# A state-space convolution and a gated feed-forward layer on one core: dummy matmuls at the start, first loads on two queues, memsets off GpSimd, a 78-row tile, another order

## The chip, the cores and the metric

The kernel runs on one core of a Trainium2 chip. The core has a matrix engine (TensorE, in the profile PE for matmuls and PEld for weight loads), a vector engine (VectorE, DVE), a scalar engine (ScalarE, ACT), GpSimd (POOL) and a sync engine (SyncE, SP) that mostly issues DMAs. Each engine takes its instructions in program order and waits on semaphores for the others. SP, ACT and GpSimd each have a DMA queue. Matmuls read SBUF and write PSUM; here PSUM is used as four double banks of 128 x 2 x 512 fp32, called banks 0 to 3 below.

The metric is the device time of one execution in microseconds (us), as the median of the runs. Before the change it was 275.33 us (three runs, 275.13 to 275.48).

## The reference

For `x` of 2048 x 640 (bf16) the kernel computes `g * a + (1 - g) * b`:

```python
g = sigmoid((x * gate_w).sum(-1, keepdims=True))
a = ssm_conv(x)          # u below is x
b = (gelu(x @ w_gate) * (x @ w_up)) @ w_down   # 640 -> 1728 -> 640

def ssm_conv(u):
    dt = exp(log_dt)[:, None]                  # 640 channels, 128 states each
    P = exp(dt * (A_re + 1j * A_im) * l)       # for each lag l = 0 .. 2047
    K = einsum("dn,dnl,dn->dl", C, P, dt * B).real
    y = irfft(rfft(pad(K)) * rfft(pad(u)))     # causal convolution along the length
    return y + u * Dskip
```

The lags are rounded to bf16 in the reference, and the kernel uses that: only a few distinct lags are left above 256.

## The kernel before

The kernel is one long hand-made schedule. Each piece of work is registered under a short name by `step(name, fn)`, and the string `ORDER` (lines 39 to 91) lists all 984 names in the order in which they are emitted. Since every engine takes its own instructions in the order of emission, `ORDER` fixes the order on each engine and on each DMA queue. A name with `/0` to `/3` opens a matmul job in that PSUM bank, and a name with `/A` or `/D` says whether ACT or DVE evacuates the bank. A job that opens in a bank waits until the readers of the job before it in that bank are done.

What the names stand for, in the rough order of the work:

- *Parameters.* `lp0` to `lp5` load A_re, A_im, C_re, C_im, B_re, B_im (L272), `ldt` the log step sizes (L268), `lpk` a constant table `picks` with an identity, two flipped identities and an edge table (L267). `t0` to `t5` turn the six parameters with ten small matmuls each (L312: the parameter is the stationary operand, 64 columns of the identity move). `tdt` (L318) spreads the log step sizes over the partitions with a matmul of one row. `dt` (ACT, L332) is the exponential of that; `al`, `al2` and `th` (DVE, L334, L335, L337) are the scaled real and imaginary exponents; `c2`, `c3` (ACT, L341) copy C out of PSUM, and `v0` to `v18` and `mag` combine B, C and A into the coefficient of each state, in magnitude and angle.
- *Tables of powers*, once for each half of the channels (suffix `.0` and `.1`). `xa`, `xb` are exponentials on ACT (L470, L472, L480, L484). `fa`, `fb`, `qa`, `qb` are phases on DVE (L492, L500, L487), `sa`, `sb` sines on ACT (L504, L507), `ma`, `pa`, `pc`, `pb` products on DVE. `oa` and `ob` are memsets of ones in these tables, `fil` two fills. `ct0.0` to `ct0.6` contract the tables over the states on PE (L537, L538), and `ek` steps unload the result. `ks`, `kd`, `kt` add the skip term and regroup the kernel samples through DRAM.
- *Gate and up products.* For each half of the length (`.0`, `.1`) there are 27 jobs `g`, `u` and `h` of ten matmuls with 512 columns (L391). In the first half the first four `g` and `u` jobs of the first two weight slots are cut by the five tiles of x (`g0.0`, `g0.0k1` to `g0.0k4`), so that they can run as the transposing loads `x0.0` to `x4.0` (L287) land. `lw0g`, `lw0u` and so on load the weights (L280). `eg`, `eu` evacuate, `su`, `sg` store to DRAM, because the results are needed only later. `hz0`, `hz1` set the lower half of the last tile of H to zero (GpSimd memsets of 64 x 1024, L622 and L630), which must follow the store `su13.0` of what lay there.
- *Folds.* `ul`, `ur` load chunks of x forwards and backwards (`ur` with GpSimd's indirect DMA, L375), `uf` adds and subtracts them (L382).
- *Spectra.* `U` and `K` jobs are the forward transforms of x and of the kernel (L729, L742), `m`, `s`, `y` the products on DVE (L788, L790, L791), `I` the inverse transform (L802).
- *The end.* `ge`, `dg` are gelu on ACT (L709, L712, L680); `rl`, `hm` reload the up products and multiply. `D` jobs are the down product, 14 tiles of rows deep (L816), `Z` mixes in the convolution (L823, L824), `o` scales and writes out (L402, L404), `st` stores. `lwz0`, `lwz1` are GpSimd memsets that clear rows 64 to 127 of the last tile of the down weights, and `lwe` writes fourteen edge rows into it. `gf` flips the gate with a table in `picks`.
- *Dummies.* `wm0` to `wm2` at the very end run two matmuls each on `picks` (L296), while the last stores are under way.

The head of the order, and its end, before:

```
lpk lp3 t3/2 ldt lp0 one tdt/1 tabE dt c3 lp5 t0/0 al lp2 t2/1 xa11.0 c2 al2 xb5.0 xb9.0 lp4 xa17.0 xb14.0 lw0g t5/0 v2 v3
xb23.0 x0.0 t4/1 g1.0/3 xa3.0 sk v0 v4 lp1 xb2.0 lw0u xa8.0 xb31.0 xb8.0 x1.0 v1 v5 v6 t1/0 th g0.0/2 u1.0/1 fb1.0 g0.0k1
x2.0 u0.0/0 idx xb21.0 g1.0k1 qb1.0 v7 xa16.0 x3.0 v8 v11 xb11.0 xa9.0 u0.0k1 u0.0k2 x4.0 v9 u0.0k3 g0.0k2 fb0.0 qb0.0 xb10.0
...
D120a D121/0 Z120 o120/A D121a D131/3 Z121 y130 D131a st120 y131 o121/A I131/0 st121 I130/1 eI131/A eI130/A Z131 o1311/D
o1310/A st1311 Z130 o1300/D st1310 o1301/A st1300 wm0/2 wm1/0 st1301 wm2/2
```

Of the kernel before, what the change touches and what calls it, by code (L numbers as in the profile page):

```python
# [39 lines left out]
lpk lp3 t3/2 ldt lp0 one tdt/1 tabE dt c3 lp5 t0/0 al lp2 t2/1 xa11.0 c2 al2 xb5.0 xb9.0 lp4 xa17.0 xb14.0 lw0g t5/0 v2 v3  # L40
xb23.0 x0.0 t4/1 g1.0/3 xa3.0 sk v0 v4 lp1 xb2.0 lw0u xa8.0 xb31.0 xb8.0 x1.0 v1 v5 v6 t1/0 th g0.0/2 u1.0/1 fb1.0 g0.0k1
x2.0 u0.0/0 idx xb21.0 g1.0k1 qb1.0 v7 xa16.0 x3.0 v8 v11 xb11.0 xa9.0 u0.0k1 u0.0k2 x4.0 v9 u0.0k3 g0.0k2 fb0.0 qb0.0 xb10.0
u0.0k4 g1.0k2 v10 xb1.0 xa4.0 u1.0k1 u1.0k2 lw1g xb29.0 ul0 eu0.0/D g0.0k3 xb3.0 u1.0k3 v12 xb15.0 v13 xb12.0 lw1u g1.0k3
u1.0k4 g1.0k4 xa15.0 eu1.0/D g3.0/0 v14 g0.0k4 g3.0k1 g3.0k2 xa14.0 xb7.0 g3.0k3 oa.0 xb17.0 u3.0/1 eg1.0/D ur0 xb6.0 su0.0
eg0.0/D xa10.0 xb19.0 g2.0/3 xa7.0 u2.0/2 xa5.0 x0.1 g3.0k4 v15 xb13.0 xa19.0 g2.0k1 xb4.0 xa1.0 v16 uf0.0 u3.0k1 uf0.1 lw2
xb27.0 xb25.0 u2.0k1 u3.0k2 v17 u2.0k2 g2.0k2 mag ma2.0 eg3.0/A u2.0k3 u3.0k3 fil.0 ma1.0 g2.0k3 su1.0 ur1 u2.0k4 v18 ma3.0
eu2.0/D g2.0k4 x2.1 us0 u3.0k4 lw3 u4.0/0 ma4.0 ma5.0 ma0.0 tabT sb0.0 fb2.0 eu3.0/A su3.0 sb1.0 ul1 pb0.0 pc0.0 eg2.0/A
su2.0 fb3.0 u5.0/2 ob.0 eu5.0/A qb2.0 sb2.0 pb1.0 g5.0/1 pc1.0 eg5.0/A fb4.0 g4.0/3 pc2.0 pb2.0 u6.0/2 eu4.0/A at qb4.0
# [96 lines left out]
def kernel(  # L145
# [125 lines left out]
    for i in range(6):  # L271
        step(f"lp{i}", lambda i=i: (A if i == 0 else S).dma_start(out=at["prm"][:, i],  # L272
                                                                 in_=PRM[i].rearrange("(p j) n -> p (j n)", p=128)))
# [628 lines left out]
```

## Time and profile before

| | |
|---|---|
| median of 3 runs | 275.33 us (275.13 to 275.48) |
| the profiled execution | 275.08 us |
| its span, first to last instruction | 273.3 us |
| busy: PE, DVE, ACT, GpSimd | 261.3, 255.6, 219.4, 36.7 us |
| DMA moved | 49.05 MB, mean 179 GB/s |
| granted TensorE clock, mean | 1.000 |

The profile is of one execution. PE's busy time is modelled, because matmuls are pipelined: a matmul that stands in the profile with 379 ns is followed by the next one after some 0.22 us, so a busy PE is read from the spacing of its instructions. "Idle before" an instruction is the time its engine did nothing before it, with the name of what ended the wait. A name such as `ps` stands for all tiles of that name. SPq, ACTq and POOLq are the engines' instruction queues, where DMAs are issued.

### The profile page before, as it was taken

How to read it: one execution, taken by the hardware profiler on the slowest of the kernel's cores; microseconds unless marked ns; L12 is line 12 of the kernel's file. 1: busy time of each engine (PE TensorE's matmuls, PEld its weight loads, DVE VectorE, ACT ScalarE, POOL GpSimd, SP SyncE). 2: the span in 40 equal slices, each digit the busy share in tenths (PEclk: the TensorE clock that was granted, in tenths of full speed). 3: DMA queues.
4: the chain of work that ended last, by engine and by line, in shares of the span. 5: the costliest groups of instructions: out<-in, count | busy, mean ns of one | idle time of the engine just before them, and what ended most of it. 6: DMA issues, size and time to landing. Idle time of an engine off the chain costs nothing.

```text
span 273.3 us, 4927 instructions
## 1 busy us (share of the span) xinstructions
PE 261.3 (96%) x1874; PEld 159.8 (58%) x1889; DVE 255.6 (94%) x330; ACT 219.4 (80%) x300; POOL 36.7 (13%) x23
## 2 busy tenths in 40 slices
...
GB/s 196 261 184 227 250 140 242 276 208 105 195 272 139 233 265 245 246 287 210 276 288 121 280 252 195 289 202 267 262 246 23 50 0 26 46 2 50 24 50 48
DMA packets 64141, 49.05 MB, mean 179 GB/s; under 512 B 23499, under 2 KB 52982, under 8 KB 64118
## 3 DMA queue, kind: packets, MB, share of 16 engines
...
q8 instruction: 15, 0.25, 0.4%
...
## 4 chain that ended last, share of the span: by engine, by line
PE 71%; ACT 18%; DVE 5%; issue 3%; DMA 2%; SPq 0%; DVEq 0%; ACTq 0%
PE ps L391 24%; PE ps L816 22%; PE ps L802 6%; PE ps L729 6%; PE ps L742 4%; ACT work L396 3%; DVE work L398 2%; ACT work L480 2%; PE ps L537 2%; PE ps L538 2%; ACT work L472 2%; ACT H L709 2%; PE ps L823 2%; ACT work L484 2%; PE ps L824 1%
## 5 line engine op out<-in xcount | busy, mean ns | idle before, releaser
L391 PE MATMUL ps<-xT,Wr 128*128 128x512 bf16 x525 | 118.9, 379 | 3.7 <-DVE work L347 0.7
L391 PEld LDWEIGHTS <-Wr 128*128 128x128 bf16 x540 | 52.6, 98 | 65.7 <-issue 5.0
L396 ACT CAST work<-ps 128x640 bf16<-128x640 f32 (+1 forms) x59 | 47.5, 838 | 11.5 <-PE ps L802 7.4
L375 POOL DMA_INDIRECT early<-in_A_u_dram,back x8 | 31.4, 3929 | 40.7 <-DVE early L382 32.3
L816 PE MATMUL ps<-xT,H 128*128 128x320 bf16 x224 | 32.9, 299 | 0.0
L402 ACT ACTIVATE Wr<-ps,gs 128x320 bf16<-128x320 f32 x30 | 14.0, 527 | 23.0 <-PE ps L824 14.7
L816 PE MATMUL ps<-xT,work 128*128 128x320 bf16 x224 | 32.4, 299 | 0.0
L816 PEld LDWEIGHTS <-H 128*128 128x128 bf16 x224 | 21.9, 98 | 8.5
L816 PEld LDWEIGHTS <-work 128*128 128x128 bf16 x224 | 21.9, 98 | 8.5
L504 ACT ACTIVATE tail<-work 128x1920 bf16<-128x1920 int16 x14 | 25.3, 1821 | 0.4
L525 DVE TENSOR_TENSOR work<-tail,work 128x1920 bf16<-128x1920 bf16 (+1 forms) x22 | 23.4, 1087 | 0.0
L507 ACT ACTIVATE tail<-work 128x1920 bf16<-128x1920 int16 (+1 forms) x12 | 19.5, 1631 | 1.5 <-DVE work L487 1.0
L802 PE MATMUL ps<-work,tail 128*128 128x320 bf16 x128 | 19.5, 299 | 0.0
L492 DVE SCALAR_TENSOR_TENSOR work<-early,tail 128x320 int32<-128x320 f32 x42 | 18.0, 481 | 0.0
L788 DVE TENSOR_TENSOR work<-work,early 128x2560 bf16<-128x2560 bf16 x12 | 17.8, 1481 | 0.0
L788 DVE TENSOR_TENSOR work<-work 128x2560 bf16<-128x2560 bf16 x12 | 17.8, 1480 | 0.0
L729 PEld LDWEIGHTS <-early 128*128 128x128 bf16 x128 | 12.5, 98 | 7.6 <-issue 2.3
L516 DVE TENSOR_TENSOR work<-tail,work 128x1920 bf16<-128x1920 bf16 x14 | 16.1, 1150 | 0.2
L487 DVE TENSOR_SCALAR work<-work 128x960 int32<-128x960 int16 (+1 forms) x26 | 16.1, 624 | 0.1
L398 DVE CAST work<-ps 128x1024 bf16<-128x1024 f32 x13 | 15.7, 1212 | 0.0
L742 PE MATMUL ps<-KTt,early 128*128 128x320 bf16 x80 | 15.5, 299 | 0.0
L802 PEld LDWEIGHTS <-tail 128*128 128x128 bf16 x128 | 12.5, 98 | 4.9
(128 smaller groups left out, 423.1 us busy)
## 6 DMA issues: line engine op xcount, KB each, us to landing
...
```

Of the source, the lines that this page charges most:

```text
L375: G.indirect_dma_start(out=at["ur"][:, e, :], out_offset=None, in_=u2[:, :], in_offset=bass.IndirectOffsetOnAxis(ap=back[:, 2 * c + e:2 * ...
L391: P.matmul(t[:, x, :], lhsT=Wr[:, slot, kt, cols:cols + 128], rhs=xT[:, th, kt, 512 * x:512 * x + 512], start=(kt == 0), stop=(kt == 4))
L396: A.copy(out=out, in_=in_)
L398: V.tensor_copy(out=out, in_=in_)
L504: act(out=T, in_=low16(t)[:, :, :, ::2], func=ACT.Sin, scale=SIN_SCALE)
L507: act(out=T[:, :, 0:n], in_=low16(t[:, :, 0:n])[:, :, :, ::2], func=ACT.Sin, scale=SIN_SCALE)
L525: tt(out=B2[:, :, :, cols].rearrange("p r g x -> p g r x"), in0=Tv if hf == 0 else Tv[:, :, ::-1], in1=e, op=ALU.mult)
L729: P.matmul(t[:, r, 0:W2], lhsT=FM[:, m, e, r], rhs=pm[:, r, e], start=(e == 0), stop=(e == 1))
L742: P.matmul(t[:, r, 0:W2], lhsT=mat[:, r], rhs=KTt[:, q, d], start=(x == 0 and j != 1), stop=(x == len(seq) - 1), skip_group_check=(j == 1))
L788: step(f"s{h}{c}{i}{part}", lambda t=t, dst=dst, op=op: tt(out=fl(dst), in0=fl(dst), in1=fl(t), op=op))
L802: P.matmul(t[:, r, 0:W2], lhsT=IM[:, e, m, r], rhs=Y[:, r, m], start=(m == 0), stop=(m == 3))
L816: P.matmul(t[:, x, 0:W2], lhsT=H[c // 2][:, ft, tk:tk + 128], rhs=at[f"Wd{h}"][:, ft], start=(ft == 0), stop=False)
```

## The change

- *Dummies.* `WARM` goes from 3 to 8, and each dummy is now one matmul of 128 x 128 on 512 columns of zeros. The zeros are a slice of H0, cleared by DVE at the start (`wmz`). The dummies stand between the parameter turns instead of at the end.
- *First loads.* The first loads take the queue from `ORDER`: `lp0`, `lp1`, `lp3`, `lp5` and the weights on SP, `ldt`, `lp2`, `lp4` on ACT. Of `picks` only the identity is loaded at the start (`lpi`, 128 of 400 columns, on ACT); the rest (`lpk`) follows late, on SP.
- *Step sizes.* `tdt` comes first, reads `ldt` in a straight line and writes PSUM with a stride, instead of the other way round.
- *Memsets.* `one`, `oa`, `ob` go from GpSimd to DVE. `hz0` and `hz1` become a scaled copy on ACT over the 14 rows 64 to 77 (`clear`). `lwz0` and `lwz1` are gone.
- *Last down tile.* The last of the 14 row tiles of the down product uses 78 rows instead of 128, in 32 matmuls.
- *Order.* `ORDER` is new throughout. Eleven evacuations go from DVE to ACT (`eu2.0`, `eu12.0`, `eu6.1`, `ek0.0`, `ek0.4`, `ek1.2`, `ek1.3`, `eU000`, `eK001`, `eK002`, `eK011`) and eleven from ACT to DVE (`eg2.0`, `eg3.0`, `eu10.1`, `ek0.1`, `ek0.2`, `ek0.3`, `ek1.0`, `ek1.1`, `ek1.6`, `eK013`, `eU003`); of the four last outputs three are now DVE's (`o1301`, `o1300`, `o1310`) and one ACT's; before it was two each.

The diff, with `ORDER` cut to its head, two places in the middle and its end:

```diff
+WARM = 8
 LATE = (8, 9, 10, 11)
-WARM = 3
...
+wmz wm1/0 lp0/S wm7/3 lp1/S lpi oa.0 lp3/S ldt/A lp2/A wm2/1 tabE one lp5/S tdt/0 dt x0.0 t0/1 t1/0 t2/2 t3/3 lp4/A ob.0 al
+xb27.0 xa4.0 t5/1 al2 th sk fb0.0 xb21.0 lw0g/S c2 v3 wm5/2 xb7.0 c3 xa19.0 v2 x1.0 t4/3 v0 wm6/1 xa8.0 lw0u/S wm0/2 g0.0/2
+v1 g0.0k1 wm4/1 x2.0 x3.0 v4 xa9.0 lw1g/S v5 xb9.0 xb13.0 xb14.0 v6 x4.0 wm3/1 qb0.0 v7 g1.0/1 xb31.0 xb4.0 xa5.0 u1.0/0
+u0.0/3 v8 ul0 lw1u/S v9 u1.0k1 xb1.0 v11 v10 fb1.0 qb1.0 g0.0k2 g1.0k1 idx g1.0k2 v12 v13 xb29.0 xa17.0 xb12.0 xa3.0 ur0 x1.1
...
+pa5.0 e13.0/A u9.0/1 sa6.0 pa6.0 ct0.0/2 lu00 uf2.1 uf2.0 eu12.0/A fb0.1 ct0.5/3 ek0.5/D fb1.1 eg12.0/A su12.0 eu9.0/A tabE2
+ct0.3/0 ct0.4/1 ct0.2/3 ek0.0/A su13.0 ek0.4/A ek0.3/D hz0 ct0.1/2 us2 qb0.1 su9.0 ek0.2/D ul3 ct0.6/1 xa4.1 ek0.1/D xa14.1
...
+eU012/A U010/0 g9.1/2 hm1.0 eU010/A kd.1 K022/1 rl3.0 lpk/S ge3.0 rl4.0 m0000 ge11.0 dg9 hm13.0 y000 m0100 m0110 eK022/A
+m0101 g10.1/0 rl11.0 dg10 hm3.0 lu02 lim0 lu03 rl5.0 gf/3 U022/2 lkb0 y001 gf1 hm11.0 K023/3 m0111 eK023/A U023/1 U021/0
...
+st121 s1301 y130 y131 I130/2 I131/1 eI130/A eI131/A Z130 o1301/D st1301 o1300/D st1300 Z131 o1311/A st1311 o1310/D st1310
...
+    queue = {"S": S, "A": A}
-    step("lpk", lambda: A.dma_start(out=picks[:], in_=nc.inline_tensor(pkc, "picks_c").ap()))
-    step("ldt", lambda: S.dma_start(out=ldt[:], in_=A_log_dt.rearrange("(o d) -> o d", o=1)))
-    step("one", lambda: G.memset(ones[:], 1.0))
+    PKd = nc.inline_tensor(pkc, "picks_c").ap()
+    step("lpi", lambda: A.dma_start(out=picks[:, 0:128], in_=PKd[:, 0:128]))
+    step("lpk", lambda q="S": queue[q].dma_start(out=picks[:, 128:400], in_=PKd[:, 128:400]))
+    step("ldt", lambda q="S": queue[q].dma_start(out=ldt[:], in_=A_log_dt.rearrange("(o d) -> o d", o=1)))
+    step("one", lambda: V.memset(ones[:], 1.0))
...
-    def warm(j):
-        for x in range(2):
-            P.matmul(PS[bank[j]][:, x, 0:400], lhsT=ident, rhs=picks[:, 0:400], start=True, stop=True)
...
-            P.matmul(t[:, h, 0:W2], lhsT=ones[:], rhs=ldt[:, W2 * h:W2 * h + W2].rearrange("o (w g) -> o g w", w=4),
+            P.matmul(t[:, h, 0:W2].rearrange("p (g w) -> p w g", w=4), lhsT=ones[:], rhs=ldt[:, W2 * h:W2 * h + W2],
                      start=True, stop=True)
...
+    zero = H0[:, 0, 0:512]
+
+    def turn_over(job):
+        P.matmul(PS[bank[job]][:, 0, :], lhsT=zero[:, 0:128], rhs=zero, start=True, stop=True)
+
+    step("wmz", lambda: V.memset(zero, 0.0))
+    for x in range(WARM):
+        step(f"wm{x}", lambda j=f"wm{x}": turn_over(j), f"wm{x}", True)
...
-        step(f"oa.{h}", lambda: G.memset(PQ[:, 1, 0], 1.0))
-        step(f"ob.{h}", lambda: G.memset(B2[:, 1, :, 60:64], 1.0))
+        step(f"oa.{h}", lambda: V.memset(PQ[:, 1, 0], 1.0))
+        step(f"ob.{h}", lambda: V.memset(B2[:, 1, :, 60:64], 1.0))
...
+    def clear(h):
+        act(out=H[h][64:78, 13], in_=picks[64:78, 0:1].to_broadcast([14, 1024]), func=ACT.Copy, scale=0.0)
+
     tables(0)
-    step("hz0", lambda: G.memset(H[0][64:128, 13], 0.0))
+    step("hz0", lambda: clear(0))
...
-    step("hz1", lambda: G.memset(H[1][64:128, 13], 0.0))
+    step("hz1", lambda: clear(1))
...
-        step(f"lwz{h}", lambda h=h: G.memset(at[f"Wd{h}"][64:128, 13], 0.0))
...
-                        P.matmul(t[:, x, 0:W2], lhsT=H[c // 2][:, ft, tk:tk + 128],
-                                 rhs=at[f"Wd{h}"][:, ft], start=(ft == 0), stop=False)
+                        rows = 128 if ft < 13 else 78
+                        P.matmul(t[:, x, 0:W2], lhsT=H[c // 2][0:rows, ft, tk:tk + 128],
+                                 rhs=at[f"Wd{h}"][0:rows, ft], start=(ft == 0), stop=False)
```

More of the change, by code (lines that the diff above doesn't have):

```diff
@@ L39 @@
 ORDER = """
[L40 to L48, printed above, removed]
@@ L78 @@
-y020 ge3.1 eK103/A eK100/A K110 Z011 rl6.1 U102/1 hm6.1 rl9.1 rg12.1 m0301 ge12.1 rl4.1 st000 eK110/A lu11 K113 hm9.1 hm4.1
-m0311 rl8.1 K102/0 rl12.1 m0310 o011/A eU102/A rl1.1 eK113/A U112/3 eU112/A hm8.1 I020/1 eK102/A er3 eI020/A K121/3 eK121/A
-K112 eK112/A lu12 st001 U113/2 eU113/A U110/1 eU110/A I021/3 K122/0 eK122/A eI021/A K123/1 st011 U111/2 rl2.1 hm12.1 U122/0
-eU111/A K101/3 eU122/A hm1.1 lwz1 U120/2 K120/0 eK123/A lwe1 eU120/A rl0.1 rl3.1 s0311 s0310 hm2.1 eK101/A lu13 hm0.1 eK120/A
```

91 lines of the change are left out of this document (46 added, 45 removed).

## Prediction

> **What bounds the kernel now.** I read the page's first part, then the busy time by stages, then the timeline of the first 24 us. The profiled execution took 275.08 us, of which 273.3 us are the span, so 1.78 us lie around it. The median of the three runs is 275.33 us, 0.25 us above the profiled one. The sum below is made on the span, and the gain is then taken off the median. About 0.2% (0.55 us) is what a measurement of this kernel can tell from no change.
>
> ```profile
> span 273.3 us, 4927 instructions
> PE 261.3 (96%) x1874; PEld 159.8 (58%) x1889; DVE 255.6 (94%) x330; ACT 219.4 (80%) x300; POOL 36.7 (13%) x23
> ```
>
> PE and DVE are both over 90% busy and ACT is at 80%. Such shares are averages, so the next view cuts the span. Each row gives a stretch, its length, then busy time and number of instructions of PE, PEld, DVE, ACT and POOL.
>
> ```profile
> 0.00:7.10 7.10, 3.67 (x25) 2.43 (x26) 0.00 (x0) 2.50 (x3) 1.48 (x8) 1.00 0.74 194
> 7.10:15.00 7.90, 6.38 (x48) 4.88 (x47) 6.86 (x10) 7.07 (x16) 2.07 (x2) 1.00 1.19 267
> 15.00:70.00 55.00, 54.08 (x246) 24.40 (x250) 54.73 (x92) 53.83 (x64) 26.05 (x4) 1.00 0.75 200
> 70.00:80.00 10.00, 9.95 (x179) 7.71 (x179) 8.50 (x11) 9.48 (x11) 2.50 (x4) 1.00 0.82 223
> 80.00:135.00 55.00, 54.09 (x327) 26.58 (x332) 54.92 (x90) 53.57 (x68) 3.31 (x5) 1.00 0.83 246
> 135.00:161.00 26.00, 23.84 (x267) 16.21 (x267) 25.94 (x35) 25.97 (x32) 0.95 (x1) 1.00 0.79 221
> 161.00:265.00 104.00, 103.95 (x761) 74.34 (x760) 103.57 (x96) 64.56 (x109) 0.36 (x1) 1.00 0.40 121
> ```
>
> From 15 to 265 us PE is idle for 4.09 us (0.92, 0.05, 0.91, 2.16, 0.05) and DVE for 2.34 us, 1.50 of it from 70 to 80 us. ACT is full until 161 us too, and half idle after that. So three engines run as a braid, and only two kinds of time are to be had: idle time in the first 15 us, and the few microseconds in which one strand waits for another. From 161 us on PE and DVE are both full, so what is not won by then isn't won any more.
>
> The head, in the timeline (start, length, engine, line, operation, count, and in brackets the idle time before it and who ended it):
>
> ```profile
> 0.75 0.40 SPq L272 DMA_DIRECT2D early<-in_A_C_im_dram  x1
> 0.76 0.36 ACTq L267 DMA_DIRECT2D picks<-picks_c  x1
> 1.21 0.32 SPq L268 DMA_DIRECT2D work<-in_A_log_dt_dram  x1
> 3.39 1.53 SPq L287 DMA_TRANSPOSE xT<-in_A_u_dram  x1
> 3.43 1.25 PE L312 MATMUL ps<-picks,early 128*128 128x64 bf16 x10 [3.43 <-DMA early<-in_A_C_im_dram]
> 4.61 1.24 PE L318 MATMUL ps<-work,ones 1*128 1x320 bf16 x2
> 5.78 4.55 PE L312 MATMUL ps<-picks,early 128*128 128x64 bf16 x40
> 5.89 0.70 ACT L332 ACTIVATE early<-ps 128x640 bf16<-128x640 f32 x1 [2.96 <-PE ps L318]
> 6.06 6.57 SPq L287 DMA_TRANSPOSE xT<-in_A_u_dram  x4
> 7.14 0.82 DVE L334 TENSOR_TENSOR tail<-ps,early 128x640 f32<-128x640 f32 x1 [7.14 <-PE ps L312]
> 8.00 0.47 ACT L470 ACTIVATE work<-tail 128x320 bf16<-128x320 f32 x1 [0.83 <-DVE tail L334]
> 9.36 0.82 DVE L348 TENSOR_TENSOR work<-ps,early 128x640 f32<-128x640 f32 x1 [0.86 <-PE ps L312]
> 10.09 0.67 PE L391 MATMUL ps<-xT,Wr 128*128 128x512 bf16 x1
> 14.88 9.22 PE L391 MATMUL ps<-xT,Wr 128*128 128x512 bf16 x41 [0.57 <-DVE early L337]
> ```
>
> The first parameter lands and is turned (L312, ten matmuls) at 3.43, `tdt` (L318) runs behind it, `t0` behind that, and `al` (L334), the first DVE work, starts at 7.14. PE's main stream (L391) runs without holes only from 14.88, when DVE has read the last banks. By the order eight of its matmuls (`g1.0`, `g0.0`, `u1.0`, `g0.0k1`) are done by then.
>
> **The head, changed.** *tdt.* It becomes PE's first work on data. `ldt` is second on ACT's queue, behind 0.36 us of issue for a third of the picks, so it is issued near 1.15, as early as on SP now (1.21). The nearest landing is the first parameter's: issued at 0.75, read at 3.43, so 2.68 us. That puts `tdt` at 3.4 to 3.8; I take 3.5. Its two matmuls took 1.24 us with a strided moving operand. Now that operand is contiguous and the output strided instead. If the stride was the price they take half, otherwise the same: 0.6 to 1.2 us, and I take 0.6, since the turns, too, write with a stride. Then `dt` (0.70 us) ends near 5.0, and `t0`, right behind `tdt`, near 5.2 (forty turns filled 5.78 to 10.09, so 1.08 us for ten). `al` starts at 5.4 instead of 7.14: 1.7 us won, 1.2 if `tdt` stays slow.
>
> *The turns.* DVE now has `al`, `al2`, `th` and `fb0` in a row, 0.82 + 0.49 + 0.82 + 0.80 = 2.9 us by the rows of L334, L335 and L500, `th` taken like `al`, until 8.3. Then `v3` needs `t5`, which stands behind `t0` to `t3`: five times 1.08 us from 4.1 is 9.5, and 0.2 to the end of the last. So DVE idles 1.4 us, where today `v2` waited 0.86 (L348). Net head gain of DVE: 1.7 - 0.5 = 1.2 us.
>
> ```profile
> 8.00 0.49 DVE L335 TENSOR_SCALAR tail<-tail 128x640 f32<-128x640 f32 x1
> 14.86 0.80 DVE L500 TENSOR_SCALAR work<-early 128x320 int32<-128x320 f32 x3
> L312 PE MATMUL ps<-picks,early x60: 247/348/348, 3.4 to 11.9; 128*128 128x64 bf16 x60
> L391 PE MATMUL ps<-xT,Wr x54: 376/379/667, 10.1 to 25.8; 128*128 128x512 bf16 x54
> xT<-in_A_u_dram SPq DMA_TRANSPOSE x10, 5.0
> ```
>
> *The dummies.* The tile rows for the first 26 us (min/median/max in ns) say that the array was slow until then: a turn took 348 and at best 247, an L391 took 667 at 10.09 and 379 as a rule. The granted clock in the stage rows is 1.00 throughout, so this is read from durations alone. Three dummies run before `tdt` on an idle PE. `wm5` stands before `t4`, within the wait for DVE. `wm6` in bank 1 is a new wait: it needs `v2`, which ends at 9.7 + 2 x 0.82 = 11.3, and behind it in PE's queue stand `wm0` and `g0.0` with the whole stream. At 0.22 us each on the fast array `g0.0` starts near 11.9; `wm4` and `wm3` add 0.44. That the array is fast near 12, as before, I take from the turns' row, whose best is 247 ns and whose last starts at 11.9. So the stream starts, in effect, at 12.3; before it was 14.88 less eight times 0.219 = 13.1. PE wins 0.8 us. The 0.219 is 10.74 / 49, from the chain:
>
> ```profile
> 44.89 10.74 PE ps L391 x49
> 265.55 2.34 PE L802 MATMUL ps<-work,tail 128*128 128x320 bf16 x16
> 263.98 0.82 DVE L791 TENSOR_TENSOR work<-work 128x1280 bf16<-128x1280 bf16 x1
> 270.00 0.53 ACT L402 ACTIVATE Wr<-ps,gs 128x320 bf16<-128x320 f32 x1 [0.36 <-DVE Wr L404]
> ```
>
> *Loads.* On SP the five parameters, `ldt` and `lw0g` stood before x0; now four parameters do, so x0 is issued near 2.6 instead of 3.39. x4's issue ends near 12.1 (1.53 + 6.57 for the five, plus `lw0g`, `lw0u` and `lw1g` at about 0.45). With 5 us from issue to landing (last row above) it is there by 17 at the latest. PE needs it after fifteen steps of 0.44 us from 12.3, at 19, so this costs nothing while the stream starts after 10.4. `lp4` is issued on ACT behind `dt`, near 5.1, and at 2.7 to 5.0 us to land is there by 10.1, in time for `t4`. The back gathers start earlier on POOL and use the same DMA engines, within that same cover.
>
> **The memsets.** GpSimd's are these, beside the evacuation rows that set the other swaps:
>
> ```profile
> L564 POOL MEMSET work<- 128x320 bf16 x2 | 0.7, 362 | 6.8 <-issue 6.8
> L398 DVE CAST work<-ps 128x1024 bf16<-128x1024 f32 x13 | 15.7, 1212 | 0.0
> L398 DVE CAST early<-ps 128x1008 bf16<-128x1008 f32 x3 | 3.6, 1203 | 0.8 <-PE ps L538 0.8
> L404 DVE TENSOR_SCALAR early<-ps 128x640 bf16<-128x640 f32 x3 | 2.4, 815 | 0.0
> L396 ACT CAST work<-ps 128x1024 bf16<-128x1024 f32 x23 | 22.9, 1015 | 0.3 <-PE ps L391 0.3
> DVE early L398 <- PE ps L538: 0.8, 2, 0.6
> PE ps L729 <- ACT tail L396: 0.6, 1, 0.6
> ```
>
> `wmz`, `one`, `oa.0`, `ob.0` run on DVE before `al`, when it is idle: nothing. `oa.1` and `ob.1` fall into its full stream: two operations, 0 to 0.36 us each (the GpSimd row), 0.2 taken: +0.4. `hz1` on ACT falls into its idle stretch: nothing. `hz0` on ACT, 1024 columns, costs 1.0 like a copy, in ACT's full stretch. It also waits for the store `su13.0` to have read that tile, and ACT's second-half exponentials are queued behind it. The store is issued two copies ahead, so I take no further wait; if the store is late, 1 us more. The two `lwz` memsets waited for PE on an engine that nobody needed: nothing. `lpk`, the rest of the picks, moves to SP between `rl3.0` and `rl4.0`, and `gf` on PE needs it; three jobs of 2.2 us stand between, so nothing.
>
> **The new order.** Eleven evacuations go from DVE to ACT (three of 1024 columns, four table parts, four of 640 columns: 3 x 1.21 + 4 x 1.20 + 4 x 0.82 = 11.7 us) and eleven back (3, six table parts, one of them 0.9, and 2: 3.6 + 6.9 + 1.6 = 12.1): DVE +0.4, ACT about -0.4. Of DVE's 1.50 us idle at 70 to 80, waits for the contraction (L538) for the most part, I take half away, since folds and phases now stand between the table copies: -0.7 (0 to -1.5). The new order of spectra and matmuls after 161 us moves work within full engines.
>
> **The 78 rows.** 32 matmuls stream as many columns as before: nothing taken; the price if not is below.
>
> **The end.** Of the last four outputs DVE now has three and ACT one, where it was two each; they ran one after the other anyway (ACT's last waited 0.36 us for DVE), the last store follows them, and the trailing dummies lay in the shadow of the stores: 0 within 0.1.
>
> **The sum.** DVE: -1.2 + 0.4 + 0.4 - 0.7 = -1.1 us, with 0.75 us to spare at the end (y131 done at 264.80, its reader at 265.55). ACT: first exponential at 6.3 instead of 8.00, less 0.2 of waiting for `c2` and `c3`, so -1.5 + 1.0 - 0.4 = -0.9 until 161 us. PE: -0.8 of its own, and its waits from 15 to 161 us (4.04 us, for ACT as in the last row above, and DVE) shrink by what these two come earlier in the head beyond PE (1.2 and 1.5 against 0.8), about 0.5: -1.3. PE carries the end but waits for ACT on the way; between -1.3 and ACT's -0.9 I take **-1.2**: span 272.1, median 275.33 - 1.2 = **274.1 us**. The unknowns above (`tdt` +0.5, memsets and `hz0` +1, table waits -0.8 to +0.7) make 273.3 to 275.2 of it.
>
> **Rivals.**
> A, *the dummies make the array fast early*. With more matmuls from 1.2 us on, `t1` to `t5` would run at half their time (the row's 247 and 348 ns are the two states; an L391 goes from 667 to 379). `t5` is done by 7.5, DVE's 1.4 us idle goes, `v2` ends at 9.9, `g0.0` starts 1.4 earlier. DVE and PE win 1.4 more; ACT, which gains by `c2` and `c3` alone, gives 0.2 of that and holds some of the rest back: -1.2 - 0.9, **273.2 us**. Against it: the turns kept PE issuing from 3.43 on, and at 10.09 it was still slow. For it: a pair of wide matmuls stands at 10.09, just before it turned fast, and the dummies are as wide. [...]
>
> B, *the start comes earlier, the end doesn't*: the array stays slow for 2 to 3 us past 12, which costs half of that, or ACT stands at `hz0` for 1 us more, and what the head wins is waited away before 161 us. 275.33 - 1.2 + 1.0 to 1.5, **275.1 to 275.6 us**.
>
> C, *the order removes waits of PE beyond mine* between 80 and 161 us (3.07 us idle now): 2 us more, **272.1 us**.
>
> D, *slower*: a matmul with fewer rows than its neighbours may have to wait for them. The only one in the trace is `tdt`, with one row: its start came 1.18 us after `t3`'s although ten turns take 1.08, so 0.1 per change, 0.2 in and out. 32 times 0.2 = 6.4 us on a PE that is full from 161 us: 275.33 - 1.2 + 6.4 = **280.5 us**. It decides from 1.2 / 32 = 38 ns each. Against it: `tdt` also waits for data, which may be all of the 0.1. [...]
>
> **Chances.** Forecast 0.44, A 0.18, C 0.08, B 0.20, D 0.10. Faster: 0.41 + 0.18 + 0.08 = 0.67. Same (274.8 to 275.9): 0.03 of the forecast and 0.14 of B, 0.17. Slower: 0.06 of B, where both its causes come together, and D, 0.16. Range: from a little above C, 272.4, to B's upper end with 0.2 for the runs' own spread, 275.8; that leaves out D and most of C.
>
> **What would show it.** `al` near 5.4 and not 7.14; DVE's wait for `t5`, 1.4 us; L391 dense from 12; the DVE idle of 70 to 80 us halved; ACT's first exponential near 6.3. A is right if the turns' median falls below 300 ns, D if L816's row of even starts has a hole at every fourteenth matmul. The forecast is wrong if PE's idle time from 80 to 161 us grows by more than 1 us.

## The result, and the profile after

The changed kernel took 277.25 us (median of six runs, 276.93 to 278.22); the kernel before took 275.11 us beside it (275.06 to 275.48). The ratio is 1.0079, with a 95% interval of 1.0062 to 1.0096: slower by 0.8%, or 2.1 us, where 274.1 us (272.4 to 275.8) and "faster" were forecast. The profiled execution took 276.93 us, with a span of 275.1 us. Medians below leave out executions in a slower state, over 1.5% above the fastest of the same kernel; there are two, both of `fil_early_best` (278.20 and 278.77 us).

The page's first part and the busy time by stages, of after:

```profile
span 275.1 us, 4926 instructions
PE 262.4 (95%) x1891; PEld 158.7 (58%) x1891; DVE 257.7 (94%) x338; ACT 220.5 (80%) x300; POOL 16.9 (6%) x14
...
0.00:7.10 7.10, 5.34 (x32) 3.22 (x33) 2.38 (x7) 2.50 (x4) 0.97 (x6) 1.00 0.71 180
7.10:15.00 7.90, 7.12 (x59) 4.39 (x57) 7.23 (x12) 7.89 (x16) 2.07 (x2) 1.00 1.20 290
15.00:70.00 55.00, 54.51 (x252) 24.51 (x251) 54.77 (x91) 54.57 (x65) 11.18 (x4) 1.00 0.78 201
70.00:80.00 10.00, 8.21 (x171) 6.88 (x170) 7.92 (x13) 7.71 (x9) 2.69 (x3) 1.00 0.68 215
80.00:135.00 55.00, 54.91 (x336) 26.90 (x335) 54.07 (x87) 54.28 (x71) 0.00 (x0) 1.00 0.79 232
135.00:161.00 26.00, 23.90 (x267) 16.17 (x265) 25.88 (x35) 25.97 (x31) 0.00 (x0) 1.00 0.86 256
161.00:265.00 104.00, 102.55 (x747) 72.74 (x746) 102.62 (x95) 65.66 (x109) 0.00 (x0) 1.00 0.41 119
```

Up to 15 us PE is busy for 2.4 us more than before, some of it with dummies, and it stays ahead until 70 us. From 70 to 80 us it is idle for 1.79 us (before 0.05), and from 161 to 265 us for 1.45 us (before 0.05). DVE, whose idle time from 70 to 80 us was to be halved, has 2.08 us of it there (before 1.50). The head won time; two later places lost more.

The head, in the timeline of after, and the tile row of the turns:

```profile
3.22 1.22 PE L314 MATMUL ps<-work,ones 1*128 1x320 bf16 x2 [0.56 <-DMA work<-in_A_log_dt_dram]
4.37 4.58 PE L308 MATMUL ps<-picks,early 128*128 128x64 bf16 x50
5.73 0.82 DVE L339 TENSOR_TENSOR tail<-ps,early 128x640 f32<-128x640 f32 x1 [3.78 <-PE ps L308]
6.59 0.47 ACT L485 ACTIVATE work<-tail 128x320 bf16<-128x320 f32 x1 [1.41 <-DVE tail L339]
9.05 0.82 DVE L354 TENSOR_TENSOR work<-ps,early 128x640 f32<-128x640 f32 x1 [0.40 <-PE ps L308]
9.49 0.72 PE L308 MATMUL ps<-picks,early 128*128 128x64 bf16 x10 [0.33 <-ACT early L346]
10.66 0.59 PE L329 MATMUL ps<-H 128*128 128x512 bf16 x2 [0.46 <-DVE work L353]
12.38 3.83 PE L396 MATMUL ps<-xT,Wr 128*128 128x512 bf16 x17
...
L308 PE MATMUL ps<-picks,early x60: 216/334/348, 4.4 to 10.0; 128*128 128x64 bf16 x60
```

`al` starts at 5.73 (before 7.14), ACT's first exponential at 6.59 (8.00), DVE waits only 0.40 us for `t5`, and PE's stream is dense from 12.38.

To follow a gain through the kernel I use one more number. For each PE job I add up the work of all jobs ahead of it at the dense spacing of the matmuls (0.216 us for 512 columns, 0.136 for 320, 0.038 for 84), and subtract that from the job's start. This **lag** is all that PE has lost up to there; the whole work is 249.98 us. One profile of each kernel:

| lag in us, after so much own work | 5 | 40 | 64 | 90 | 140 | 160 | 249 |
|---|---|---|---|---|---|---|---|
| time in after, us | 16 | 52 | 79 | 105 | 158 | 180 | 269 |
| before | 12.94 | 14.05 | 14.33 | 14.86 | 18.55 | 18.62 | 18.70 |
| after | 11.31 | 12.30 | 14.59 | 14.83 | 18.01 | 19.79 | 20.42 |
| uf2_late | 12.16 | 13.71 | 14.13 | 17.41 | 21.09 | 22.43 | 22.69 |
| two_waits | 11.11 | 12.14 | 12.56 | 13.85 | 17.00 | 17.47 | 18.84 |
| two_waits_no_dummies | 10.84 | 12.96 | 13.39 | 14.67 | 17.85 | 18.31 | 20.14 |
| new_code_old_order | 12.67 | 13.94 | 15.15 | 15.23 | 18.91 | 19.00 | 19.65 |
| before_two_waits | 13.15 | 14.27 | 20.32 | 20.86 | 24.50 | 26.39 | 26.46 |
| fil_early | 12.34 | 13.32 | 14.14 | 14.06 | 17.25 | 18.05 | 18.31 |

After is 1.75 us ahead of before when 40 us of work are done. It loses 1.86 us at one job, `ct0.1` (77 us), and 1.58 us at another, behind `U100` (170 us), and ends 1.72 us behind.

**The first loss.** GpSimd's timeline and DVE's folds, of before (with two lines of DVE ahead of them that are needed further down), then of after, and of after a line of its waits:

```profile
69.37 0.64 DVE L512 TENSOR_TENSOR work<-work,tail 128x960 bf16<-128x960 bf16 x1
70.12 2.42 DVE L516 TENSOR_TENSOR work<-tail,work 128x1920 bf16<-128x1920 bf16 x2
46.80 24.04 POOL L375 DMA_INDIRECT early<-in_A_u_dram,back  x1 [16.77 <-DVE early L382]
71.15 0.95 POOL L375 DMA_INDIRECT early<-in_A_u_dram,back  x1 [0.30 <-issue]
74.42 1.55 DVE L382 TENSOR_TENSOR early<-early 128x1280 bf16<-128x1280 bf16 x2
```

```profile
60.75 8.05 POOL L380 DMA_INDIRECT early<-in_A_u_dram,back  x1 [31.92 <-DVE early L387]
69.11 1.61 POOL L380 DMA_INDIRECT early<-in_A_u_dram,back  x1 [0.30 <-issue]
73.05 1.56 DVE L387 TENSOR_TENSOR early<-early 128x1280 bf16<-128x1280 bf16 x2 [2.08 <-DMA early<-in_A_u_dram,back]
...
PE ps L542 <- DVE early L403: 1.7, 1, 1.7
```

The fold `uf2.1` needs the rows that the gather `ur2` brings. Before, they were there when the order came to it. In after it stands right behind the last table product, finds the rows missing and holds DVE for 2.08 us; behind it in DVE's queue stand the copies that free PSUM, so the contraction waits 1.7 us. The gather itself is odd: it has two parts, and the first takes 24.04 us in before and 8.05 in after, where every other part of a gather takes 0.94 to 1.61 us in these two traces.

**The second loss.** SyncE's issue of `lu10` in before, its issue in after, and the matmul that reads it:

```profile
160.90 0.53 SPq L754 DMA_DIRECT2D tail<-PMd  x1
```

```profile
164.43 0.54 SPq L761 DMA_DIRECT2D tail<-PMd  x1
169.85 0.70 PE L736 MATMUL ps<-tail,early 128*128 128x320 bf16 x4 [1.42 <-DMA tail<-PMd]
```

The load is issued 3.5 us later, three jobs ahead of its reader, and PE, with nothing else to do in this stage, stands for 1.42 us.

### The profile page after: what moved, and what is told of

It reads as the page before. It is cut to its first block, busy times and chain, and to the rows that moved or that the text cites. A ratio compares the mean times of both kernels' runs of the same rounds, so it can differ in the third digit from the quotient of the medians.

```text
span 275.1 us, 4926 instructions
## 1 busy us (share of the span) xinstructions
PE 262.4 (95%) x1891; PEld 158.7 (58%) x1891; DVE 257.7 (94%) x338; ACT 220.5 (80%) x300; POOL 16.9 (6%) x14
## 4 chain that ended last, share of the span: by engine, by line
PE 55%; ACT 10%; DMA 2%; issue 2%; DVE 0%; DVEq 0%; ACTq 0%
PE ps L824 22%; PE ps L396 16%; PE ps L809 6%; PE ps L736 5%; PE ps L749 4%; ACT H L716 3%; ACT tail L509 2%; DMA tail<-PMd 2%; ACT work L401 2%; PE ps L831 1%; PE ps L832 1%; ACT early L407 1%; ACT tail L401 1%; ACT work L688 1%; DVE Wr L409 0%
## 5 line engine op out<-in xcount | busy, mean ns | idle before, releaser
L401 ACT CAST work<-ps 128x640 bf16<-128x640 f32 (+1 forms) x61 | 50.2, 851 | 19.6 <-PE ps L832 8.5
L824 PE MATMUL ps<-xT,H 128*128 128x320 bf16 (+1 forms) x224 | 33.1, 299 | 0.0
L824 PEld LDWEIGHTS <-H 128*128 128x128 bf16 (+1 forms) x224 | 21.9, 98 | 8.5
L380 POOL DMA_INDIRECT early<-in_A_u_dram,back x8 | 15.9, 1992 | 59.6 <-DVE early L387 51.3
L542 PE MATMUL ps<-work 128*128 128x84 bf16 x160 | 12.4, 199 | 2.7 <-DVE early L403 1.7
```

What stands on the lines that cost most here:

```text
L401: A.copy(out=out, in_=in_)
L824: P.matmul(t[:, x, 0:W2], lhsT=H[c // 2][0:rows, ft, tk:tk + 128], rhs=at[f"Wd{h}"][0:rows, ft], start=(ft == 0), stop=False)
```

## Experiments

Theory 1: two waits that the new order made ate the head's gain. Theory 2: the code edits did (memsets on full engines, 78 rows). Times are medians; in brackets the interval of the ratio to the kernel before, which took 275.1 to 275.2 us beside each.

### One wait at a time

`uf2_late`, `lu10_early`, and `both` with the two edits together; all edits in this part are moves of names in `ORDER`:

```diff
-... ct0.0/2 lu00 uf2.1 uf2.0 eu12.0/A ... ek0.3/D hz0 ct0.1/2 us2 ...
+... ct0.0/2 lu00 eu12.0/A ... ek0.3/D hz0 ct0.1/2 uf2.1 uf2.0 us2 ...
```

```diff
-... dg11 rg4.1 m0211 ... eU030/A lu10 ge13.1 ...
+... dg11 rg4.1 lu10 m0211 ... eU030/A ge13.1 ...
```

> The changed kernel (277.25 us), in which only the two folds uf2.1 and uf2.0 stand later on VectorE, behind the last table copies, just ahead of the store us2. Theory 1 (order): the 2.08 us in which VectorE waited for the gather ur2 go, the contraction's 1.70 us with them; TensorE's lag behind its own work at 80 us falls by 1.5 to 1.9 us and the time comes to 275.3 to 275.8 us. Rival (the code edits cost it: hz0 on ScalarE, the memsets on VectorE, 78 rows): the wait goes but something else is late in its place, and the time stays at 276.8 to 277.6 us.

> The changed kernel, in which only the load lu10 stands earlier on SyncE's queue, right behind rg4.1, ahead of the loads that wait for er0. Theory 1: U100 no longer waits its 1.42 us, and the stage from 161 us on, where TensorE has nothing left to hide a wait behind, ends that much earlier: 275.7 to 276.2 us. Rival: the wait is taken back later by the full VectorE, ScalarE and TensorE of that stage, and under 0.5 us of it reaches the end: 276.8 to 277.3 us.

> Both moves, uf2.1 and uf2.0 later and lu10 earlier, in the changed kernel. Theory 1: the two gains add, 2.9 to 3.4 us, and the time is 273.8 to 274.5 us, under the kernel before (275.1 us). Rival: 276.5 us and more.

Measured: uf2_late 278.31 us [1.0074 to 1.0122], lu10_early 276.87 [1.0055 to 1.0081], both 279.05 [1.0121 to 1.0151]. Theory 1's numbers failed. Of the five executions of lu10_early the profiled one is the fastest (275.35 us); the median is only 0.4 us under the changed kernel. The lag of uf2_late at 64 says that its wait did go, and the next column that 3.3 us are lost behind it. SyncE's issues of after and of uf2_late, with two lines of the latter's waits, say why:

```profile
74.64 0.34 SPq L388 DMA_DIRECT2D PMd<-early  x1
76.52 0.81 SPq L282 DMA_DIRECT2D Wr<-in_B_w_gate_dram  x1
```

```profile
79.03 0.34 SPq L388 DMA_DIRECT2D PMd<-early  x1
80.90 0.81 SPq L282 DMA_DIRECT2D Wr<-in_B_w_gate_dram  x1
...
PE ps L396 <- DMA Wr<-in_B_w_gate_dram: 1.5, 1, 1.5
PE ps L396 <- DVE early L403: 1.1, 1, 1.1
```

The store `us2` waits for the fold on SyncE's queue, and the weights `lw8` stand behind it: moving the fold 4.4 us moved the weights 4.4 us, and PE waited 1.5 us for them. The second line is a copy of a table part that follows the fold on DVE in its new place; PE waited 1.1 us for the bank that it frees. I had moved a step without its DMAs and without looking at what stands behind it.

`two_waits` is both moves, with the fold only as late as `ek0.3` and with `us2` and `ul3` behind `lw8`; `before_two_waits` puts the same two steps into bad places of the kernel before:

```diff
-... ek0.4/A ek0.3/D hz0 ct0.1/2 us2 qb0.1 su9.0 ek0.2/D ul3 ... qb1.1 lw8 xb13.1 ...
+... ek0.4/A uf2.1 uf2.0 ek0.3/D hz0 ct0.1/2 qb0.1 su9.0 ek0.2/D ... qb1.1 lw8 us2 ul3 xb13.1 ...
```

```diff
-... ma6.0 pa6.0 g11.0/3 ... lw7 uf2.1 tabE2 uf2.0 ...
+... ma6.0 pa6.0 uf2.1 uf2.0 g11.0/3 ... lw7 tabE2 ...
-... lu10 hm3.0 ... I000/0 U031/1 hm0.0 K021/3 dg10 rl9.0 m0210 U103/2 ...
+... hm3.0 ... I000/0 lu10 U031/1 hm0.0 K021/3 dg10 rl9.0 m0210 U103/2 ...
```

> The changed kernel with uf2.1 and uf2.0 some 2 to 4 us later on VectorE (ahead of ek0.3), and the store us2 and the load ul3 behind lw8 on SyncE's queue, so that a late store holds up no weight load; lu10 stands early, behind rg4.1. Theory 1 (two waits made by the order ate the head's gain): 1.5 to 2 us from 70 to 80 us and 0.4 to 1.4 us at 170 us, not given back at 88 us: 274.0 to 275.2 us. Rival (the stages behind are full and every saving is waited away by another order-made wait): 276.3 us and more.

> The kernel before with two of the changed kernel's places: uf2.1 and uf2.0 right behind pa6.0, the last table product, and lu10 only three jobs ahead of U103, its first reader. Theory 1: the contraction waits 1.5 to 2 us at 72 us and U103 1 to 1.5 us at 166 us, and the time is 277.3 to 278.7 us. Rival: both waits are filled by other work and the time is 275.0 to 275.7 us.

Measured: two_waits 275.73 us [1.0012 to 1.0037], between the two expectations, 1.5 us under the changed kernel and still 0.6 above the one before. By the table it loses 1.29 us between 64 and 90 us of own work, where the changed kernel loses 0.24: there, too, PE waits 0.9 us for table copies that follow the fold in its new place. before_two_waits took 283.1 us [1.0273 to 1.0326], so +8.0 where 2 to 3.5 were expected. (In it one product, `pa5.0`, still stands behind the fold.) DVE's wait in before_two_waits, and its stages:

```profile
74.33 1.56 DVE L381 TENSOR_TENSOR early<-early 128x1280 bf16<-128x1280 bf16 x2 [2.83 <-DMA early<-in_A_u_dram,back]
```

```profile
74.00:76.00 2.00, 0.00 (x0) 0.00 (x0) 1.67 (x3) 0.29 (x1) 0.00 (x0) 1.00 0.87 187
78.00:80.00 2.00, 2.00 (x34) 2.00 (x31) 0.92 (x3) 0.75 (x1) 0.00 (x0) 0.50 0.38 134
80.00:82.00 2.00, 2.00 (x40) 2.00 (x38) 0.00 (x0) 1.97 (x3) 0.00 (x0) 0.65 0.68 146
```

The contraction waited 4.1 us, and then the granted clock (the column after POOL's) fell to 0.50: the trace's clock record has 3.41 us at half speed. So a wait of 4 us cost 6 (lag 14.27 to 20.32). `U103` lost 1.9 us more. Both places are dear, as theory 1 said.

### Code or order

`new_head_old_order`: the changed code with its order up to the turns, then the order of before (banks 1 and 3 exchanged). `new_code_old_order`: the changed code, with the order of before from the start and no dummies. The second try of the first, `..._2`, differs in one name, and new_code_old_order has it there as well:

```diff
-... K012 eK012/A ... rl1.0 lpk/S gf/1 ...
+... lsk lpk/S ma6.0 ...
```

> The changed kernel's code and its order up to the last turn (dummies, loads on two queues, memsets on VectorE, hz0 and hz1 on ScalarE, 78 rows), and from there the order of the kernel before, with banks 1 and 3 exchanged and the rest of picks loaded late. Theory 1: the head's gain of 1.4 to 1.8 us reaches the end and the code edits cost under 0.4 us: 273.3 to 274.2 us. Rival (the code edits or the earlier head eat the gain): 275.0 us and more.

> As new_head_old_order, with the rest of picks loaded at 60 us, behind lsk, not at 148 us where TensorE waited 3.6 us for it. Theory 1 (the changed kernel's loss is in its order from 70 us on): 279.75 less the 3.6 us wait and some 1.5 us of the clock that fell behind it is 274.2 to 274.9 us, under the kernel before. Rival (the new code or the early head costs elsewhere): 275.5 us and more.

> The changed kernel's code with the whole order of the kernel before: lp0 and the 32 KB of picks first on ScalarE's queue, the other loads on SyncE's, memsets on VectorE, hz0 and hz1 on ScalarE, 78 rows, no dummies at the head and none at the end. Theory 1: the code edits are worth within 0.5 us of nothing, 274.6 to 275.6 us. Rival (memsets on full engines and 78 rows cost on the path): 276.0 us and more. If the early picks alone bring the head's gain: 273.7 to 274.4 us.

Measured: 279.75 us [1.0139 to 1.0172], 275.86 [1.0015 to 1.0037] and 276.18 [1.0021 to 1.0047]. The first was my own mistake: `gf` waited 3.6 us for the late `lpk`, and the clock fell again, as the stages of new_head_old_order say:

```profile
154.00:156.00 2.00, 2.00 (x7) 0.71 (x5) 2.00 (x4) 1.80 (x2) 0.00 (x0) 0.51 0.99 360
156.00:158.00 2.00, 2.00 (x7) 0.79 (x6) 2.00 (x4) 2.00 (x2) 0.00 (x0) 0.64 0.02 7
```

With that mended, theory 1's forecast for this kernel still fails, and new_code_old_order says that the new code costs 1.1 us in the old order, so theory 2 has a share. The trace of new_code_old_order shows two places. At 78 us, within `ct0.4`, PE has two holes between matmuls of 38 ns that nothing else explains ("issue" is time in which the engine waited for nothing that the profile shows); a line of its waits, 70 to 82 us:

```profile
PE ps L542 <- issue: 0.6, 2, 0.4
```

At `ct0.4` the lag is 0.12 us below that of before, at the next job, `h.1`, 0.83 above. Before and after have no such hole. And from 187 to 195 us it rises by 0.5 us against before: `hz1` (1.05 us) now stands on ACT at 184.13 us. The stage from 183 to 197 us, of before and of new_code_old_order:

```profile
183.00:197.00 14.00, 14.00 (x105) 10.09 (x104) 13.87 (x18) 13.44 (x23) 0.00 (x0) 1.00 0.89 270
```

```profile
183.00:197.00 14.00, 13.99 (x102) 9.70 (x101) 13.88 (x18) 13.93 (x24) 0.00 (x0) 1.00 0.90 271
```

ACT, half idle from 161 us on as a whole, is busy here for 13.44 of 14.00 us, so a memset of 1.05 us finds 0.56. Both places are read off one trace; no run moves them one at a time.

### The head's parts

Three single edits of two_waits: without the dummies (`wmz`, `wm0` to `wm7`), with `lp4` on SyncE, and with the memsets on GpSimd (14 rows for `hz0`, `hz1`):

```diff
-... lp5/S tdt/0 dt x0.0 ... t3/3 lp4/A ob.0 ...
+... lp5/S lp4/S tdt/0 dt x0.0 ... t3/3 ob.0 ...
```

```diff
-        act(out=H[h][64:78, 13], in_=picks[64:78, 0:1].to_broadcast([14, 1024]), func=ACT.Copy, scale=0.0)
+        G.memset(H[h][64:78, 13], 0.0)
```

> two_waits (275.73 us) without the eight dummy matmuls and the memset ahead of them. Theory 1: the dummies are what makes the array fast at 8 us and not at 11 to 12 us; without them the turns and the first matmuls are 1.0 to 1.6 us later and the end with them: 276.6 to 277.3 us. Rival (the later stages are full on VectorE and ScalarE and take such a gain back anyway): 275.5 to 276.2 us.

> two_waits with the parameter load lp4 sixth on SyncE's queue again, as before, and not on ScalarE's, where it is issued at 4.4 us, behind an instruction that waits for the first turn. Theory: the turn t4 came 0.4 to 1.3 us late by that load, more in one execution than in the next, and this spreads the times (274.59 to 276.88 us); with lp4 early the median falls by 0.3 to 0.8 us to 274.9 to 275.4 us and the spread to under 1 us. Rival: the six loads share the same engines, the load lands no earlier, 275.5 to 276.0 us and the same spread.

> two_waits with the memsets back on GpSimd: one, oa, ob (they stand on VectorE in the changed kernel) and the zeroing of 14 rows of the last tile, hz0 and hz1 (1.05 us of ScalarE each). Theory 2 (the new homes of the memsets cost on the full engines): 0.3 to 0.8 us are gained, 274.9 to 275.4 us. Theory 1 (they are beside the path): 275.5 to 275.9 us.

Measured: 276.61 us [1.0032 to 1.0072], 276.0 [1.0018 to 1.0049], 276.0 [1.0013 to 1.0042]. The dummies are worth 0.9 us; the lag at 40 us of own work is 12.96 without them, 12.14 with. The queue of `lp4` and the homes of the memsets change nothing that can be told in this order, and the spread stays at 2 us and more.

### What holds the gather

Sixteen of the twenty traces have a long gather (16.61 us in uf1_early, about 24.04 us in the five with the old order, about 8.05 us in the other ten), and in all of them it ended 0.71 to 0.80 us behind DVE's first hole after its start. In before DVE ran without one from 46.80 us; then came 104 ns of idle time ahead of the instruction at 70.12 us (the two DVE lines above: 69.37 and 0.64 make 70.01), and at 70.84 the gather was done. In after the hole is 35 ns long, at 68.01, between the two instructions of `fil.0`, and the gather ends at 68.81. `uf1_early` starts the gather earlier; `fil_early` moves the hole alone:

```diff
-... lw3 ... us0 ... pc1.0 g5.0/2 ... uf1.1 ... uf1.0 ... us1 ul2 ur2 ...
+... lw3 us0 ... pc1.0 uf1.1 uf1.0 ur2 g5.0/2 ... us1 ul2 ...
```

```diff
-... lw6 uf1.0 g11.0/1 ... us1 ul2 ur2 fil.0 lw7 ...
+... lw6 uf1.0 fil.0 g11.0/1 ... us1 ul2 ur2 lw7 ...
```

> The changed kernel with the folds uf1.1 and uf1.0 at 39 us on VectorE (they stood at 54 and 60 us), so that the gather ur2, which needs their buffer, can start at 40 us instead of 60.75 us; the store us0 stands ahead of them; uf2, lu10 and the rest are where the changed kernel has them. Theory 1a (the gather was only started late): both halves of it are done by 45 us, uf2.1 waits no more, and the time is 275.3 to 275.9 us. Theory 1b (GpSimd's gather does not get on while VectorE runs without a hole, from 45 us to 68 us): it takes 15 us and more, ends near 70 us as before, uf2.1 waits again for 1.5 to 2.2 us, and the time stays at 276.9 to 277.6 us.

> The changed kernel with only fil.0 moved: two short VectorE instructions (L534) between which every trace so far has a hole of 34 or 35 ns; they stood at 67.7 us and now stand at 61 us, right behind uf1.0, ahead of which the gather ur2 starts at 60.75 us. No work is added or taken away. Theory H (the gather gets on only in a hole of VectorE: it ended 0.72 to 0.80 us behind the first hole in five traces): it now ends at 61.8 to 62.5 us, not at 68.81, the rows are there by 68 us, uf2.1 waits no more, and of the 1.86 us that TensorE loses at 77 us at least 1.3 go: 275.4 to 275.9 us. Rival (it takes 8 us for a reason of its own, or the later stages take the gain back): 276.9 to 277.6 us.

Measured: uf1_early 275.33 us [0.9996 to 1.0017], fil_early 274.68 [0.9969 to 1.0002]. In uf1_early the fold of chunk 1 uses the reversed rows of chunk 0, because that move also put it ahead of `ur1`, and `ur2` now runs ahead of `ur1`, which overwrites its rows; as a timing it still answers half the question. The slow gather in it is `ur2` again. GpSimd in uf1_early, then GpSimd, the fold and the stage from 70 to 80 us in fil_early:

```profile
40.30 16.61 POOL L380 DMA_INDIRECT early<-in_A_u_dram,back  x1 [29.35 <-DVE early L387]
```

```profile
61.78 1.02 POOL L380 DMA_INDIRECT early<-in_A_u_dram,back  x1 [31.93 <-DVE work L534]
63.11 1.32 POOL L380 DMA_INDIRECT early<-in_A_u_dram,back  x1 [0.30 <-issue]
72.30 1.55 DVE L387 TENSOR_TENSOR early<-early 128x1280 bf16<-128x1280 bf16 x2
```

```profile
70.00:80.00 10.00, 9.51 (x178) 7.52 (x176) 9.71 (x15) 9.64 (x11) 1.97 (x2) 1.00 0.57 181
```

Started at 40.30, the gather crawled for 16.61 us, until 0.79 us behind a hole of 34 ns at 56.12: an early start did not make it shorter. But both gathers were done by 62.87 us, the fold at 72.10 did not wait, and the time is 1.9 us under the changed kernel's, within theory 1a's range. With `fil.0` beside its start the gather that took 8.05 us took 1.02. `uf2.1` did not wait, though it stands where the changed kernel has it, and 2.6 us are gone from the time by moving two instructions of 0.25 us. So the wait at this gather is the larger part of the miss; that is shown, by two edits that remove it in different ways. By the table it isn't the whole of these 2.6 us: between 40 and 64 us of own work fil_early loses 1.47 us less than the changed kernel, and between 140 and 160 another 0.98, because `lu10`, whose queue runs earlier too, makes PE wait 0.47 us there and not 1.42.

With theory H the time came out below its range (275.4 to 275.9), and its mechanism is shown only in part. In fil_early the hole (61.68 to 61.72) lies 0.06 us ahead of the gather's recorded start at 61.78, not behind it. And other gathers ran with no hole of DVE in them: those at 26.29 and 69.11 in after took 1.29 and 1.61 us, the one at 63.11 in fil_early 1.32. So a held gather was done behind a hole in all sixteen traces, which are three different placements; what decides at its start whether it is held at all, a hole just ahead or the kind of instruction that DVE runs, stays open.

The gather was held through 23.2 us of different instructions of VectorE in before and 15.8 us in uf1_early, and was done behind one hole, of 104 and of 34 ns. What holds it, no run shows.

### What spreads the times, and a better version

The kernel before stays within 0.6 us from run to run; the kernels in the changed order spread over 1.1 to 3.1 us, the one without dummies too (2.0), while the new head with the old order behind it (`..._2`) spreads over 0.9. Two more profiles of two_waits, and one dummy less in fil_early:

```diff
-... t4/3 v0 wm6/1 xa8.0 ...
+... t4/3 v0 xa8.0 ...
```

> The kernel two_waits once more, for a second profile: its times lie between 274.59 and 276.88 us where those of the kernel before lie within 0.6 us. Theory S1: the head's loads land at times that differ, and TensorE's first matmuls come up to 1.3 us later in slow executions. Theory S2: it is the loads that the order issues late (lw8, lu10 and the like), and the difference arises behind 70 us. The profile that differs from the first one tells by where the lag differs.

> A third profile of two_waits, to the same end as two_waits_b: under theory S1 the lag of TensorE behind its own work differs from the first profile's at 15 us already, under S2 only behind 70 us.

> fil_early (274.68 us, 273.32 to 276.37) without one of the eight dummies, wm6, which writes the bank that the turn t5 used and so waits until VectorE has read it (0.4 to 0.9 us, more when the load of the turn lands late), with the first gate matmul g0.0 behind it. Theory S1a: this dummy is what hands the loads' spread on to TensorE; without it g0.0 comes 0.4 to 0.9 us earlier, the median is 273.9 to 274.3 us and the spread is smaller. Rival: u0.0 waits for VectorE's reads of t4 anyway, and nothing is gained: 274.5 to 274.9 us, the same spread.

Measured: 276.49 and 275.45 us (one run each; the first profile was of 275.27), and 274.74 for fil_early_no_wm6 [0.9972 to 0.9993]. The turns and DVE's `v3`, in the first profile of two_waits and in two_waits_b:

```profile
4.46 4.28 PE L308 MATMUL ps<-picks,early 128*128 128x64 bf16 x50
8.85 0.82 DVE L354 TENSOR_TENSOR work<-ps,early 128x640 f32<-128x640 f32 x1
```

```profile
4.42 5.24 PE L308 MATMUL ps<-picks,early 128*128 128x64 bf16 x50
9.76 0.82 DVE L354 TENSOR_TENSOR work<-ps,early 128x640 f32<-128x640 f32 x1 [1.07 <-PE ps L308]
```

S1 had the right place: the lag at 5 us of own work is 11.11 in the first profile, 12.02 in two_waits_b and 11.70 in two_waits_c. But the loads are not the cause: the turns start no later in two_waits_b, fifty of them just take 5.24 us and not 4.28. The trace's clock record reaches full speed at 7.26, 9.22 and 8.49 us, and over the twelve profiles of the changed order with all eight dummies the lag follows that moment: 11.03 at 7.12, 11.31 at 7.79 (after), 11.53 at 8.34, 11.95 at 9.30, 12.34 at 9.93 (fil_early). The clock column of the stage rows shows 1.00 before it as well, so the moment is read from this record alone. The unbroken stretches at full speed last 262.83 us (as in before) or 266.24 (as in after), 77 or 78 times 3.413, and among the three profiles of two_waits the moment differs by 1.96 us: by these traces the clock changes on a beat of 3.413 us that does not start with the kernel. In before full speed came at 11.88 us, and in two kernels with the old head 9.70 and 9.78, with lags of 12.94, 13.15 and 12.67: there the lag doesn't follow it. In before PE's stream began at 14.88 us behind DVE's `th`, not behind the turns. How much of the spread from run to run the clock's moment makes is not shown: most kernels have one profile.

`wm6` hands little on. Without it the lag at 5 us of own work is 10.63, with it 11.70 in two_waits_c, whose clock was full at the same 8.49 us; but 1.45 us of lag come back at 21 us, where PE waits for a copy on DVE. Two lines of the waits of fil_early_no_wm6:

```profile
PE ps L396 <- DVE work L403: 1.3, 1, 1.3
PE ps L736 <- DMA tail<-PMd: 1.6, 1, 1.6
```

The second is `lu10` again. The last two kernels move it, with `fil.0` early: `fil_early_best` (with the memsets on GpSimd, `wm6` kept) and `fil_lu10_no_wm6`.

> The changed kernel with fil.0 early, lu10 early (behind rg4.1) and the memsets one, oa, ob, hz0 and hz1 on GpSimd. Theory 1: both waits gone and nothing late behind them, the head's gain reaches the end: 273.3 to 274.4 us, under the kernel before (275.17 us). Rival (VectorE and ScalarE are full and take it back): 275.2 us and more.

> As fil_early_no_wm6, with lu10 early as well (behind rg4.1); hz0 and hz1 stay on ScalarE and the memsets on VectorE, as in the changed kernel. Theory 1: the wait ahead of U100 (0.63 us of lag at 168.5 us in fil_early) goes too: 0.3 to 0.7 us under fil_early_no_wm6, 273.2 to 274.0 us, a version faster than both kernels. Rival (the stage from 161 us on is full on VectorE and takes it back): the same time as fil_early_no_wm6 within 0.2 us.

Measured: 275.49 us [0.9981 to 1.0017] and 275.25 [0.9985 to 1.0017], so no gain over fil_early. In the profiles the wait is gone: lags end at 16.94 and 18.09, after starts at full clock of 7.43 and 9.95 us. The medians don't show it. The ten executions of fil_early_best fall into two groups, four from 273.52 to 274.27 us and six from 275.30 to 276.00, which no trace explains, and three of twelve executions of the last kernel had 2.57 to 2.84 us outside the span, where its others had 1.7 to 1.9. What `lu10` costs stays open: between nothing and the 1.5 us of the trace. The one version that is faster than both kernels by its interval is fil_early_no_wm6, by 0.18%, about what can be told.

## Why the prediction was wrong

- *The head* was won, and more than was forecast, but the size is in part the luck of this execution: PE is 1.75 us ahead at 52 us, not 0.8, with the clock full at 7.79; in fil_early, with the same head and the clock full at 9.93, it is 0.73 by the table. `al` at 5.73 (5.4 forecast), ACT at 6.59 (6.3). `tdt` took 1.22 us (1.24 before), so moving the stride to its output won nothing. DVE waited 0.40 us for `t5`, not 1.4, because the clock was full at 7.79, not "near 12, as before" (in after a turn started every 0.107 us up to that moment and every 0.056 us behind it), and because DVE's own chain reached `v3` 0.35 us later than forecast. That is rival A's mechanism, half of it: by its own test, a median below 300 ns, it isn't shown (334), and the moment moves by 2.8 us between the profiles of the changed order with all dummies (7.12 to 9.93).
- *Loads.* For the head's loads "this costs nothing" stands unrefuted: the one that a run moved, `lp4`, changed nothing that can be told.
- *Memsets.* In the changed order nothing, as far as 276.0 against 275.73 can tell. "`hz1` on ACT falls into its idle stretch: nothing" used the average of 161 to 265 us; in the old order the lag rises by 0.5 us at its place.
- **The step that failed** is "Of DVE's 1.50 us idle at 70 to 80 ... I take half away ...: -0.7". It was +1.86 of lag, outside the "-0.8 to +0.7" kept for table waits, and in the sum it meets PE's term: PE's waits from 15 to 161 us were to shrink by "about 0.5" and grew from 4.04 to 4.47 us, 1.74 us more from 70 to 80 us and less elsewhere. I took the idle time as something to be filled and asked what DVE waits for, not what the steps that fill it wait for. `uf2.1` needs `ur2`, whose 24.04 us stood in the trace of before, next to a fold that came just after its landing.
- *"The new order of spectra and matmuls after 161 us moves work within full engines"* left out the queue: `lu10` is issued 3.5 us later. The sum had nothing for it; in the profile it is 1.58 us, in the medians it isn't shown.
- *78 rows.* Behind each of the 32 matmuls the next one starts after 140 ns instead of 136, and the one after that after 138 or 139: 0.2 us together. Rival D is out. *The end* is within 0.1 us.
- *Rival B* said that the gain would be waited away, by clock or `hz0`, and stopped at 275.6. It was waited away, and more, by order. My test for a wrong forecast, PE's idle time from 80 to 161 us, fell from 3.07 to 2.19 us: it looked at the wrong stretches.
